# Two feed-forwards behind linear attention: the second up projection as seven block products for eight

## The chip, the cores and the metric

The kernel runs on one core of a Trainium2 chip. The metric is the device time of one execution in microseconds (us), the median of several runs. The core's engines run beside each other and each runs its own instructions in order: TensorE (PE; its weight loads are PEld), VectorE (DVE), ScalarE (ACT), GpSimd (POOL) and SyncE (SP), which issues the DMA transfers. They meet through semaphores.

## What is computed

Linear attention with a root-mean-square norm, then a gated feed-forward, then a second one with softplus:

```python
kv = np.einsum('bhsd,bhse->bhde', k, v)                  # 4 x 8 heads, 576 x 64
out = np.einsum('bhsd,bhde->bhse', q, kv)
x = (out / np.sqrt(np.mean(out * out, -1, keepdims=True) + 1e-06) * g_norm)   # 2304 x 512
g = x @ w_gate                                           # 512 x 1536
y = (g / (1 + np.exp(-g)) * (x @ w_val)) @ w_out         # 1536 x 512
h = y @ w_in                                             # 512 x 2048
z = (np.maximum(h, 0) + np.log1p(np.exp(-np.abs(h)))) @ w_out2    # 2048 x 512
```

The four weight matrices lie in DRAM as 8-byte numbers, two 4-byte words each.

## The kernel before

The 2304 tokens are five tiles: four of 512 columns, t = 0 to 3, and one of 256, t = 4 (the rest of every batch). Features lie on partitions. Every matrix product of the feed-forwards is made of three matmuls: each operand is kept as a high part and a low part in the float32r format, and `mm3` (L423) issues high by high, low by high and high by low.

Up projections contract 512 features in four steps (`up_proj`, L432: four `mm3` into one PSUM bank of the pool `ps`, five banks). Down projections go to the pool `po`, three banks, and VectorE adds each bank to an accumulator in SBUF (L486 `yacc`, L534 `zacc`); the bank is free when that add is done. In the first feed-forward `unit1(j, t)` (L624) is the unit of work: one block of 128 hidden features j (12 of them) by one token tile: four gate steps, four value steps, and between the last of these the four down steps of the unit before. Behind the value steps stands a chain: VectorE makes `u` (L465), ScalarE its high part `uh` (L468), VectorE its low part `ul` (L469); the next unit's first down step needs both. In the second feed-forward `unit2` (L635) takes two blocks j, j+1 and one token tile: 8 up steps, and 4 down steps of two blocks each, two units behind; softplus (L510) and `gh` (L511) are ScalarE's, `gl` (L512) GpSimd's.

A weight block comes by one DMA of 512 KB into one of five `stage` buffers and is turned by `split` (L253) in five steps: ScalarE L262, VectorE L265 and L266, VectorE L270, ScalarE L274, and the low part (L277) on GpSimd (first feed-forward) or VectorE (second). In the first feed-forward that is three blocks per j, in the second four per pair of j.

The order is written out by hand (`manual_schedule`): TensorE's order is that of the calls; `defer(dt, f)` puts work for the other engines into a list by planned time, and `tick` moves that time on with every `mm3` (0.216 us for a 512-column matmul) and issues what is due. So an instruction's place in its engine's row is set beforehand, at a place of TensorE's row.

## Time and profile before

| | us |
|---|---|
| median of three runs | 938.91 (938.23 to 939.47) |
| the profiled execution | 938.39 |
| its span, first to last instruction | 936.3 |
| TensorE busy | 905.9 |
| VectorE busy | 501.5 |
| ScalarE busy | 297.1 |
| GpSimd busy | 201.9 |

The span is the stretch of the profiled execution in which instructions ran; 2.1 us of its time lie around it. The first 160 us hold the loads and the attention, woven with the first two hidden blocks of the first feed-forward; from there to about 525 us the first feed-forward runs in a loop of 37 us per j, and from 525.6 to 922.9 us the second in a loop of 49 us per pair. A matmul's row shows its whole passage, 0.39 us for 512 columns, while the next one starts after 0.227 us: the distance between starts is what counts.

### The profile page before, as it was taken

To read this page: it belongs to the slowest core of one execution; us is meant where nothing else is said; L and a number is where in the kernel's file an instruction comes from. 1 tells how busy PE (TensorE), PEld (TensorE's weight loads), DVE (VectorE), ACT (ScalarE), POOL (GpSimd) and SP (SyncE) were. 2 spreads that over 40 slices of the span, in tenths; PEclk is the share of its full clock that TensorE was granted. 3 is DMA by queue.
4 is the path that set the end of the run, shared out by engine and by line. 5 is a ranking of instruction groups with operands and counts; after the bars stand their busy time and mean duration, and the time that the engine had idled before them with its cause. 6 is when DMAs were issued, how large, how long until landed. Compare 5 with 4: busy or idle time off the path is not lost.

```text
span 936.3 us, 11157 instructions
## 1 busy us (share of the span) xinstructions
PE 905.9 (97%) x4448; PEld 758.6 (81%) x4448; DVE 501.5 (54%) x805; ACT 297.1 (32%) x524; POOL 201.9 (22%) x164
## 2 busy tenths in 40 slices
PE   6899999999999999999999899999999999999994
PEld 5688887888888888888888788888888888888883
DVE  3945546665656656656657834443534443535222
ACT  3644343222222222222224633323232333233220
POOL 1722201100101111101014732222122222222220
PEclk9999999999999999999999999999999999999997
DMA  9973202201111111102010202111101020100022
...
DMA packets 58152, 55.25 MB, mean 59 GB/s; under 512 B 24692, under 2 KB 53364, under 8 KB 57716
## 3 DMA queue, kind: packets, MB, share of 16 engines
...
q14 instruction: 17, 0.14, 0.0%
q10 hardware_dynamic: 160, 0.00, 0.0%
...
## 4 chain that ended last, share of the span: by engine, by line
PE 89%; DVE 4%; SPq 2%; issue 2%; ACT 1%; DMA 1%; POOL 0%; POOLq 0%; DVEq 0%
PE pz L428 21%; PE ph L428 20%; PE pg L428 15%; PE pv L428 14%; PE py L428 14%; PE pa L358 1%; PE kvp L310 1%; DMA qr<-in_q_dram 1%; DVE yacc L486 1%; SPq L177 1%; PE px L389 1%; SPq L200 0%; PE pq L341 0%; DVE ul L469 0%; PE kvp L319 0%
## 5 line engine op out<-in xcount | busy, mean ns | idle before, releaser
L486 DVE TENSOR_TENSOR yacc<-yacc,py 128x512 f32<-128x512 f32 (+1 forms) x220 | 138.5, 631 | 98.9 <-PE py L428 98.3
L534 DVE TENSOR_TENSOR zacc<-zacc,pz 128x512 f32<-128x512 f32 x126 | 86.5, 687 | 189.0 <-PE pz L428 188.6
L512 POOL TENSOR_TENSOR gl<-l,gh 128x512 fp32r<-128x512 f32 (+1 forms) x80 | 96.6, 1208 | 280.7 <-ACT gh L511 161.7
L428 PE MATMUL ph<-yl,ih 128*128 128x512 f32 (+1 forms) x320 | 117.7, 368 | 0.0
L428 PE MATMUL ph<-yh,il 128*128 128x512 f32 (+1 forms) x320 | 117.7, 368 | 0.0
L428 PE MATMUL ph<-yh,ih 128*128 128x512 f32 (+1 forms) x320 | 117.6, 367 | 0.0
L510 ACT ACTIVATE l<-ph 128x512 f32<-128x512 f32 (+1 forms) x80 | 44.4, 555 | 228.1 <-PE ph L428 226.6
L428 PE MATMUL pz<-ph,gh 128*128 128x512 f32 x288 | 112.3, 390 | 0.0
L428 PE MATMUL pz<-pl,gh 128*128 128x512 f32 x288 | 112.3, 390 | 0.0
L428 PE MATMUL pz<-ph,gl 128*128 128x512 f32 x288 | 112.0, 389 | 0.0
L428 PE MATMUL py<-uh,oh 128*128 128x512 f32 (+1 forms) x240 | 90.3, 376 | 4.2 <-ACT uh L468 2.6
L468 ACT CAST uh<-u 128x512 fp32r<-128x512 f32 (+1 forms) x60 | 34.6, 577 | 176.6 <-DVE u L465 176.4
L428 PE MATMUL pg<-xh,gh 128*128 128x512 f32 (+1 forms) x240 | 90.1, 375 | 0.0
L428 PE MATMUL pv<-xh,vh 128*128 128x512 f32 (+1 forms) x240 | 89.8, 374 | 0.0
L428 PE MATMUL py<-ul,oh 128*128 128x512 f32 (+1 forms) x240 | 88.7, 370 | 0.8 <-DVE ul L469 0.8
L428 PE MATMUL pg<-xl,gh 128*128 128x512 f32 (+1 forms) x240 | 88.5, 369 | 0.3 <-DVE xl L396 0.3
L428 PE MATMUL py<-uh,ol 128*128 128x512 f32 (+1 forms) x240 | 88.7, 369 | 0.0
L428 PE MATMUL pv<-xh,vl 128*128 128x512 f32 (+1 forms) x240 | 88.6, 369 | 0.0
L428 PE MATMUL pg<-xh,gl 128*128 128x512 f32 (+1 forms) x240 | 88.5, 369 | 0.0
L428 PE MATMUL pv<-xl,vh 128*128 128x512 f32 (+1 forms) x240 | 88.4, 368 | 0.0
L428 PEld LDWEIGHTS ph<-yh,ih 128*128 128x128 f32 x320 | 60.2, 188 | 11.0
L428 PEld LDWEIGHTS ph<-yh,il 128*128 128x128 f32 x320 | 60.2, 188 | 10.8
...
## 6 DMA issues: line engine op xcount, KB each, us to landing
...
```

Of the source, the lines that this page charges most:

```text
L177: nc.sync.dma_start(kr.rearrange("p h c d -> p h (c d)"), ks.rearrange("h (p c) d -> p h (c d)", p=P))
L310: nc.tensor.matmul(pk[:, hp, :], lhsT=kt[:, c, i:i + 2, :].rearrange("p h d -> p (h d)"), rhs=vt[:, i:i + 2, c * D:(c + 1) * D], start=(c ...
L358: nc.tensor.matmul(pv[p0:p0 + n, hp, :], lhsT=qt[:, hp, p0:p0 + n], rhs=kvm[bb][:, hp, :], start=True, stop=True,)
L389: nc.tensor.transpose(px[:, hp, :], x[:, hp, :], ident)
L428: nc.tensor.matmul(dst, lhsT=a, rhs=b_, start=first and i == 0, stop=last and i == n - 1)
L468: nc.scalar.copy(uh, u)
L486: defer(ADD1, lambda: nc.vector.tensor_add(a[:, d, :], a[:, d, :], p))
L510: nc.scalar.activation(l, p, AF.Softplus)
L512: nc.gpsimd.tensor_sub(ul, l, f32(uh))
L534: defer(ADD2, lambda: nc.vector.tensor_add(av[:, m, :], av[:, m, :], p))
```

## The change

For each pair of hidden blocks (2jp, 2jp+1) and each pair of token tiles the second up projection is a 2 x 2 by 2 x 2 block product: the two hidden blocks by the two halves of the 512 input features (256 each), by the two token tiles. It was eight block products of 256 features; it is now seven (Strassen's scheme in Winograd's form), with sums of weight halves (`sums`), of token halves (`t_sum`) and of products. A product is `mm`: two `mm3`, six matmuls of 512 columns. Three PSUM banks X, Y, Z serve a pair: p6, p7, p3 and p4 add into a bank that already holds another product, and ScalarE (`copy`) or VectorE (`out_`) reads that bank first, in between.

The weight side: `pair2` converts the four weight blocks of a pair during the first feed-forward (j = 2 on, one pair every 40 planned us), makes four half-size sums on VectorE, and writes six blocks, high and low, to DRAM, 12 stores of 256 KB. `load2` reads them back before their use: once for tiles 0 and 1, and once more for tiles 2 and 3, since the second feed-forward now runs in two passes, n = 0 over tiles 0 and 1, n = 1 over tiles 2, 3 and the narrow one (`rest`, which keeps the plain product). The low parts are all GpSimd's.

The token side: `block` makes high (ScalarE) and low part (`BLO`: GpSimd for 0, 3, 4, 5; VectorE for 1, 2, 6) of seven 1,024-column blocks for each pair of tiles, and `t_sum` makes four sums on VectorE, in place in `yacc`. `blocks1` does that at the end of the first feed-forward in place of `yh`, `yl` of tiles 0 to 3; `blocks2` in the last pair of the first pass. The small SBUF pools become one pool `pages` of 12 buffers, plus 3 of the tag `rm`. The attention and the first feed-forward's matmuls stay.

```diff
-P2_AT = 14.36
-P2_EVERY = 8.29
-SPLIT2 = 3.88
+PAIR2 = 40.0
+STEP2 = 1.35
+LOAD2 = 8.0
...
+WLO2 = "gggggg"
+BLO = "gvvgggv"
...
-    remp = ctx.enter_context(tc.tile_pool(name="remp", bufs=1))
-    tp = ctx.enter_context(tc.tile_pool(name="tp", bufs=2))
-    cvp = ctx.enter_context(tc.tile_pool(name="cvp", bufs=2))
-    ap_ = ctx.enter_context(tc.tile_pool(name="ap", bufs=2))
+    pages = ctx.enter_context(tc.tile_pool(name="pages", bufs=12))
+    dram = ctx.enter_context(tc.tile_pool(name="dram", bufs=1, space=bass.MemoryType.DRAM))
...
-                (nc.gpsimd if YL[d] == "g" else nc.vector).tensor_sub(yl[:, d, :], a[:, d, :], f32(yh[:, d, :]))
-            if j == F1 - 1:
+                nc.gpsimd.tensor_sub(yl[:, d, :], a[:, d, :], f32(yh[:, d, :]))
...
+        def sums():
+            a, b = z["i", 0], z["i", 1]
+            z[1], z[2] = page("s12_"), page("s34_")
+            a11, a12, a21, a22 = a[:, :hw], a[:, hw:], b[:, :hw], b[:, hw:]
+            s1, s2, s3, s4 = z[1][:, :hw], z[1][:, hw:], z[2][:, :hw], z[2][:, hw:]
+            return [(s3, a11, a21, "-"), (s1, a21, a22, "+"), (s2, a22, s3, "-"), (s4, a12, s2, "-")]
...
+        def keep(i, key):
+            src = z[key]
+            hi = pages.tile([P, DM], F32R, tag="pg", name=f"kh{jp}_{i}")
+            z["h", i] = hi
+            nc.scalar.copy(hi, src)
+        def keep_lo(i, key):
+            src, hi = z[key], z["h", i]
+            lo = pages.tile([P, DM], F32R, tag="pg", name=f"kl{jp}_{i}")
+            (nc.gpsimd if WLO2[i] == "g" else nc.vector).tensor_sub(lo, src, f32(hi))
+            nc.sync.dma_start(w2d[jp][i][:, 0, :], f32(hi))
+            nc.sync.dma_start(w2d[jp][i][:, 1, :], f32(lo))
...
+        steps = conv("i", 0) + conv("i", 1) + [lambda i=i: add(i) for i in range(4)]
+        steps += kept(0, ("i", 0)) + kept(3, ("i", 1)) + kept(1, 1) + kept(2, 2)
+        steps += conv("p", 0) + kept(4, ("p", 0)) + conv("p", 1) + kept(5, ("p", 1))
+        for k_ in range(2):
+            defer(at - LOAD2 + 1.0 * k_, lambda k_=k_: load_cols(w2_in, "i", js[k_]))
+            defer(at + 10.0 + 6.0 * k_, lambda k_=k_: load_rows(w2_out, "p", js[k_]))
+        for k_, f in enumerate(steps):
+            defer(at + STEP2 * k_, f)
+    w2 = {}
+    def load2(jp):
+        for i in range(4):
+            if i < 2:
+                t = stage.tile([P, 2, DM], F32R, tag="stage", name=f"wh{jp}_{i}")
+                nc.sync.dma_start(f32(t), w2d[jp][i])
+                hl = t[:, 0, :], t[:, 1, :]
+            else:
+                hl = [wp.tile([P, DM], F32R, tag="ab"[i - 2] + "hl"[k_], name=f"wh{jp}_{i}{k_}") for k_ in range(2)]
+                for k_ in range(2):
+                    nc.sync.dma_start(f32(hl[k_]), w2d[jp][i][:, k_, :])
+            w2["h", jp, i] = hl
+        for i in range(2):
+            hl = [wop.tile([P, DM], F32R, tag="o" + "hl"[k_], name=f"wo{jp}_{i}{k_}") for k_ in range(2)]
+            for k_ in range(2):
+                nc.sync.dma_start(f32(hl[k_]), w2d[jp][4 + i][:, k_, :])
+            w2["o", jp, i] = hl
+    blk = {}
...
+    def block(n, i, tag, src):
+        def hi():
+            t = xp.tile([P, 2, KH, T], F32R, tag=tag, name=f"b{n}_{i}")
+            blk[n, i] = t
+            nc.scalar.copy(t[:, 0], src())
+        def lo():
+            t = blk[n, i]
+            (nc.gpsimd if BLO[i] == "g" else nc.vector).tensor_sub(t[:, 1], src(), f32(t[:, 0]))
+        return [hi, lo]
...
+    def t_sum(n, o, a, b):
+        def f():
+            h = halves(n)
+            nc.vector.tensor_sub(h[o], h[a], h[b])
+        return [f]
...
+    def block_steps(n, tags):
+        return [
+            block(n, 0, tags[0], half(n, 0)),
+            t_sum(n, 0, 2, 0) + block(n, 1, tags[1], half(n, 0)),
+            t_sum(n, 0, 3, 0) + block(n, 2, tags[2], half(n, 0)),
+            block(n, 3, tags[3], half(n, 1)),
+            t_sum(n, 2, 3, 2) + block(n, 4, tags[4], half(n, 2)),
+            block(n, 5, tags[5], half(n, 3)),
+            t_sum(n, 1, 1, 0) + block(n, 6, tags[6], half(n, 1)),
+        ]
+    TAGS1 = ["xh0", "xl0", "xh1", "xl1", "xh2", "xl2", "xh3"]
+    TAGS2 = ["xl3"] + TAGS1[:6]
+    def spread(steps, at, every):
+        return [(at + every * i, f) for i, f in enumerate(steps)]
+    def blocks1(t):
+        if t == 1:
+            s = block_steps(0, TAGS1)
+            blk["steps"] = s
+            return spread(s[0] + s[3], 0.5, 1.0)
+        if t == 2:
+            s = blk["steps"]
+            return spread(s[1] + s[2] + s[4] + s[5], 0.5, 0.6)
+        if t == 3:
+            return spread(blk["steps"][6], 0.9, 0.6)
+        return []
+    def blocks2():
+        s = block_steps(1, TAGS2)
+        r = spread(s[0], 0.2, 0.6)
+        for i in range(1, 7):
+            r += spread(s[i], 1.4 + 2.4 * (i - 1), 0.75)
+        return r
+    us2 = {}
+    served = count()
...
+    def quad(jp, t0, t1):
...
+        def mm(bank, i, first, a, c):
+            if first:
+                st[bank] = ps.tile([P, T], F32, tag="ps", name=f"h{bank}{jp}_{n}")
+            wh, wl = w2["h", jp, a]
+            b = blk[n, i]
+            mm3(st[bank], [
+                ((wh[:, (c + k_) * P:(c + k_ + 1) * P], wl[:, (c + k_) * P:(c + k_ + 1) * P]), (b[:, 0, k_], b[:, 1, k_]))
+                for k_ in range(KH)
+            ], first, True, check=False)
+        def copy(nm, bank):
+            st[nm] = pages.tile([P, T], F32, tag="rm", bufs=3, name=f"{nm}{jp}_{n}")
+            nc.scalar.copy(st[nm], st[bank])
+        def out_(nm, bank, other, k_, t):
+            st[nm] = page(f"{nm}{jp}_{n}")
+            nc.vector.tensor_add(st[nm], st[other], st[bank])
+            soft(2 * jp + k_, t, st[nm], st[nm], g_tiles())
+        def p1():
+            mm("Y", 0, True, 0, 0)
+            copy("p1", "Y")
+        def p5():
+            mm("Z", 1, True, 1, 0)
+            copy("p5", "Z")
+        def p6():
+            mm("Y", 2, False, 1, KH)
+            copy("u2", "Y")
+        def p2():
+            mm("X", 3, True, 0, KH)
+            out_("c11", "X", "p1", 0, t0)
+        def p7():
+            mm("Y", 4, False, 2, 0)
+            out_("c22", "Y", "p5", 1, t1)
+        def p3():
+            mm("Z", 5, False, 2, KH)
+            out_("c12", "Z", "u2", 0, t1)
+        def p4():
+            mm("Y", 6, False, 3, KH)
+            soft(2 * jp + 1, t0, st["Y"], page(f"c21{jp}_{n}"), g_tiles())
+        return [p1, p5, p6, p2, p7, p3, p4]
...
                 weave(unit1(1, t) + unit1(1, t + 1))
-        for j in range(2, F1):
-            if j + 1 < F1:
-                prepare(w1(j + 1), 10.0, P1_AT, P1_EVERY)
-            else:
-                prepare(w2(0), 12.0, 12.0, 6.0)
+        for jp in range(F2 // 2):
+            pair2(jp, jp * PAIR2)
+        for j in range(2, F1 - 1):
+            prepare(w1(j + 1), 10.0, P1_AT, P1_EVERY)
             for t in range(NT):
                 weave(unit1(j, t))
+        j = F1 - 1
+        load2(0)
+        for t in range(NT - 1):
+            weave(unit1(j, t))
+            for dt, f in blocks1(t):
+                defer(dt, f)
+        weave(ffn1_h(j, B))
         nc.scalar.preload_act_table_set("softplus")
-        behind += [[]] * (2 - LAG1)
-        for j in range(0, F2, 2):
-            if j + 2 < F2:
-                prepare(w2(j + 2), 10.0, P2_AT, P2_EVERY)
-            for t in range(NT):
-                weave(unit2(j, t))
-        for o in behind:
-            weave(o)
+        last = behind.pop(0)
+        for f in last + ffn1_o(j, B):
+            f()
+        late = []
+        for n, (t0, t1) in enumerate(((0, 1), (2, 3))):
+            for jp in range(F2 // 2):
+                if (n, jp) != (1, F2 // 2 - 1):
+                    load2((jp + 1) % (F2 // 2))
+                main = quad(jp, t0, t1)
+                if n == 0 and jp == F2 // 2 - 1:
+                    for dt, f in blocks2():
+                        defer(dt, f)
+                seq = []
+                for f in main:
+                    seq += [f] + late[:1]
+                    late = late[1:]
+                if n == 1:
+                    for f in rest(jp):
+                        seq += [f] + late[:1]
+                        late = late[1:]
+                for f in seq + late:
+                    f()
+                late = ffn2_o(jp, t1) + ffn2_o(jp, t0) + (ffn2_o(jp, B) if n == 1 else [])
+        for f in late:
+            f()
         flush()
```

Three places where the order of an engine moves. VectorE in the first feed-forward, from unit (6, 2) to (6, 3), before; `oz7` is a weight block of the first feed-forward, `py6_2_0` the first down bank of unit (6, 2):

```order
L486 TENSOR_TENSOR yacc1_875<-yacc1_875,py6_1_3_2842 128x512
L265 TENSOR_SCALAR oz7_2856<-oz7_2856 128x512
L266 SCALAR_TENSOR_TENSOR oz7_2856<-or7_2767,oz7_2856 128x512
L486 TENSOR_TENSOR yacc2_1146<-yacc2_1146,py6_2_0_2872 128x512
L270 SCALAR_TENSOR_TENSOR oz7_2856<-or7_2767,oz7_2856 128x512
L486 TENSOR_TENSOR yacc2_1146<-yacc2_1146,py6_2_1_2880 128x512
L486 TENSOR_TENSOR yacc2_1146<-yacc2_1146,py6_2_2_2889 128x512
L465 TENSOR_TENSOR u6_3_2898<-s6_3_2864,pv6_3_2866 128x512
```

The same place now; `zi8` and `zi9` are blocks of `w_in`, `s34_4` is a half-size sum:

```order
L493 TENSOR_TENSOR yacc1_918<-yacc1_918,py6_1_3_3173 128x512
L268 SCALAR_TENSOR_TENSOR zi8_3154<-ir8_3077,zi8_3154 128x512
L263 TENSOR_SCALAR oz7_3188<-oz7_3188 128x512
L264 SCALAR_TENSOR_TENSOR oz7_3188<-or7_3085,oz7_3188 128x512
L263 TENSOR_SCALAR zi9_3196<-zi9_3196 128x512
L264 SCALAR_TENSOR_TENSOR zi9_3196<-ir9_3090,zi9_3196 128x512
L493 TENSOR_TENSOR yacc2_1189<-yacc2_1189,py6_2_0_3206 128x512
L268 SCALAR_TENSOR_TENSOR oz7_3188<-or7_3085,oz7_3188 128x512
L268 SCALAR_TENSOR_TENSOR zi9_3196<-ir9_3090,zi9_3196 128x512
L493 TENSOR_TENSOR yacc2_1189<-yacc2_1189,py6_2_1_3216 128x512
L551 TENSOR_TENSOR s34_4_3231<-zi8_3154,zi9_3196 128x256
L493 TENSOR_TENSOR yacc2_1189<-yacc2_1189,py6_2_2_3226 128x512
```

Five instructions of the second feed-forward's weights now stand between the adds of these two units.

VectorE at the end of the first feed-forward (j = 11) before, from the end of unit (11, 1) on; `il0` and `iz1`, `pz0` belong to weights of the second feed-forward:

```order
L486 TENSOR_TENSOR yacc1_875<-yacc1_875,py11_1_3_4373 128x512
L277 TENSOR_TENSOR il0_4276<-iz0_4277,ih0_4275 128x512
L270 SCALAR_TENSOR_TENSOR iz1_4331<-ir1_4221,iz1_4331 128x512
L486 TENSOR_TENSOR yacc2_1146<-yacc2_1146,py11_2_0_4405 128x512
L265 TENSOR_SCALAR pz0_4397<-pz0_4397 128x512
L266 SCALAR_TENSOR_TENSOR pz0_4397<-pr0_4278,pz0_4397 128x512
L486 TENSOR_TENSOR yacc2_1146<-yacc2_1146,py11_2_1_4417 128x512
L486 TENSOR_TENSOR yacc2_1146<-yacc2_1146,py11_2_2_4430 128x512
L465 TENSOR_TENSOR u11_3_4440<-s11_3_4399,pv11_3_4401 128x512
```

The same place now; `b0_1` is a low part of a token block, the L622 rows are sums of 1,024 columns:

```order
L493 TENSOR_TENSOR yacc1_918<-yacc1_918,py11_1_3_4962 128x512
L622 TENSOR_TENSOR yacc0_644<-yacc1_918,yacc0_644 128x1024
L609 TENSOR_TENSOR b0_1_4975<-yacc0_644,b0_1_4975 128x1024
L622 TENSOR_TENSOR yacc0_644<-yacc1_918,yacc0_644 128x1024
L609 TENSOR_TENSOR b0_2_4991<-yacc0_644,b0_2_4991 128x1024
L622 TENSOR_TENSOR yacc1_918<-yacc1_918 128x1024
L493 TENSOR_TENSOR yacc2_1189<-yacc2_1189,py11_2_0_4993 128x512
L493 TENSOR_TENSOR yacc2_1189<-yacc2_1189,py11_2_1_5003 128x512
L493 TENSOR_TENSOR yacc2_1189<-yacc2_1189,py11_2_2_5014 128x512
L472 TENSOR_TENSOR u11_3_5025<-s11_3_4985,pv11_3_4987 128x512
L476 TENSOR_TENSOR ul11_3_5028<-u11_3_5025,uh11_3_5027 128x512
L493 TENSOR_TENSOR yacc2_1189<-yacc2_1189,py11_2_3_5031 128x512
```

Five 1,024-column instructions now stand ahead of the add that frees `py11_2_0`, and two more ahead of `u11_4`.

GpSimd in the second feed-forward before, where its row holds low parts of 512 or 256 columns alone:

```order
L512 TENSOR_TENSOR gl12_0_6799<-l12_0_6797,gh12_0_6798 128x512
L512 TENSOR_TENSOR gl13_0_6837<-l13_0_6835,gh13_0_6836 128x512
L512 TENSOR_TENSOR gl12_1_6875<-l12_1_6873,gh12_1_6874 128x512
L512 TENSOR_TENSOR gl13_1_6914<-l13_1_6912,gh13_1_6913 128x512
L512 TENSOR_TENSOR gl12_2_6935<-l12_2_6933,gh12_2_6934 128x512
```

GpSimd at the end of the first token pass now; `b1_0` to `b1_5` are low parts of token blocks of the second pass, `gl28` to `gl31` those of the last pair:

```order
L609 TENSOR_TENSOR b1_0_6224<-yacc2_1189,b1_0_6224 128x1024
L609 TENSOR_TENSOR b1_3_6268<-yacc2_1189,b1_3_6268 128x1024
L679 TENSOR_TENSOR gl28_6292<-c117_0_6289,gh28_6291 128x512
L609 TENSOR_TENSOR b1_4_6303<-yacc3_1314,b1_4_6303 128x1024
L679 TENSOR_TENSOR gl29_6318<-c227_0_6315,gh29_6317 128x512
L609 TENSOR_TENSOR b1_5_6313<-yacc3_1314,b1_5_6313 128x1024
L679 TENSOR_TENSOR gl30_6343<-c127_0_6340,gh30_6342 128x512
L679 TENSOR_TENSOR gl31_6364<-c217_0_6362,gh31_6363 128x512
```

The low parts that the next down projection reads now stand behind 1,024-column ones.

## Rows read from the trace of the kernel before

**Rows 1.** The page, busy time: us (share of span) xinstructions of each engine.
```profile
PE 905.9 (97%) x4448; PEld 758.6 (81%) x4448; DVE 501.5 (54%) x805; ACT 297.1 (32%) x524; POOL 201.9 (22%) x164
```

**Rows 2.** Chain that ended last, second feed-forward: start, us, engine, tile, line, matmuls.
```profile
600.40 4.08 PE ph L428 x18
...
611.28 2.15 PE ph L428 x18
```

**Rows 3.** Stretches: length, busy us (x) of PE, PEld, DVE, ACT, POOL, PEclk, DMA, GB/s.
```profile
345.00:382.00 37.00, 37.00 (x182) 31.28 (x182) 23.45 (x40) 9.22 (x16) 3.86 (x3) 1.00 0.13 43
493.00:530.00 37.00, 35.59 (x166) 28.91 (x165) 29.94 (x39) 17.90 (x32) 19.37 (x14) 1.00 0.14 43
628.00:677.00 49.00, 49.00 (x229) 41.01 (x228) 21.76 (x35) 15.83 (x28) 12.03 (x10) 1.00 0.14 43
```

**Rows 4.** Waits of TensorE from 520 us on: total us, times, longest.
```profile
PE py L428 <- DVE yacc L486: 1.6, 2, 1.3
PE py L428 <- ACT uh L468: 1.0, 1, 1.0
PE py L428 <- DVE ul L469: 0.2, 1, 0.2
```

**Rows 5.** Instructions by line and form: xcount | busy us, mean ns | idle before.
```profile
L486 DVE TENSOR_TENSOR yacc<-yacc,py 128x512 f32<-128x512 f32 x176 | 120.3, 685 | 63.4 <-PE py L428 62.8
...
L469 DVE TENSOR_TENSOR ul<-u,uh 128x512 fp32r<-128x512 f32 x48 | 34.9, 726 | 32.9 <-ACT uh L468 32.9
...
L468 ACT CAST uh<-u 128x512 fp32r<-128x512 f32 x48 | 29.8, 620 | 137.9 <-DVE u L465 137.8
...
L486 DVE TENSOR_TENSOR yacc<-yacc,py 128x256 f32<-128x256 f32 x44 | 18.2, 418 | 35.5 <-PE py L428 35.5
...
L277 POOL TENSOR_TENSOR gl<-gz,gh 128x512 fp32r<-128x512 f32 x12 | 15.6, 1297 | 181.4 <-ACT gh L274 181.4
...
L266 DVE SCALAR_TENSOR_TENSOR gz<-gr,gz 128x512 int32<-128x512 int32 x12 | 8.3, 693 | 0.4
...
L265 DVE TENSOR_SCALAR gz<-gz 128x512 int32<-128x512 int32 x12 | 5.1, 422 | 0.7 <-ACT gz L262 0.6
```

**Rows 6.** VectorE in order of time, one unit of the first feed-forward: start, us, [idle].
```profile
315.66 0.69 DVE L465 TENSOR_TENSOR u<-s,pv 128x512 f32<-128x512 f32 x1
317.04 0.69 DVE L469 TENSOR_TENSOR ul<-u,uh 128x512 fp32r<-128x512 f32 x1 [0.69 <-ACT uh L468]
317.64 0.68 DVE L486 TENSOR_TENSOR yacc<-yacc,py 128x512 f32<-128x512 f32 x1
...
320.35 0.69 DVE L486 TENSOR_TENSOR yacc<-yacc,py 128x512 f32<-128x512 f32 x1 [0.24 <-PE py L428]
321.71 0.69 DVE L486 TENSOR_TENSOR yacc<-yacc,py 128x512 f32<-128x512 f32 x1 [0.67 <-PE py L428]
...
323.82 0.69 DVE L465 TENSOR_TENSOR u<-s,pv 128x512 f32<-128x512 f32 x1
```

**Rows 7.** VectorE and GpSimd in order of time at the end of the first feed-forward.
```profile
508.06 3.07 POOL L491 TENSOR_TENSOR yl<-yacc,yh 128x512 fp32r<-128x512 f32 x2 [1.88 <-ACT yh L490]
...
508.30 1.67 DVE L266 SCALAR_TENSOR_TENSOR iz<-ir,iz 128x512 int32<-128x512 int32 x1
...
509.89 0.68 DVE L486 TENSOR_TENSOR yacc<-yacc,py 128x512 f32<-128x512 f32 x1
```

**Rows 8.** Stretches behind the last matmul, columns as in rows 3.
```profile
924.00:925.00 1.00, 0.00 (x0) 0.00 (x0) 0.00 (x0) 0.00 (x0) 0.00 (x0) 1.00 0.13 33
926.00:927.00 1.00, 0.00 (x0) 0.00 (x0) 0.00 (x0) 0.00 (x0) 0.00 (x0) 0.50 0.13 45
```

**Rows 9.** TensorE in order of time, first matmuls of the execution.
```profile
7.43 2.05 PE L310 MATMUL kvp<-v,k 128*128 128x128 f32 x8 [7.43 <-DMA v<-in_v_dram]
...
15.38 1.06 PE L310 MATMUL kvp<-v,k 128*128 128x128 f32 x8
```

**Rows 10.** One stretch of the opening loads, columns as in rows 3.
```profile
13.00:14.00 1.00, 1.00 (x6) 1.00 (x7) 0.52 (x1) 0.11 (x1) 0.00 (x0) 1.00 1.09 349
```

More of the change, by code (lines that the diff above doesn't have):

```diff
@@ L59 @@
 WLO1 = "g"
-WLO2 = "v"
 YL = "gggg"
-A0 = "v"
+WLO2 = "gggggg"
+BLO = "gvvgggv"
+GLO = "gggg"
 @with_exitstack
@@ L419, in attention_slots, with mm3 @@
         return kvs + pipe
-    def mm3(dst, steps, first=True, last=True, lo_rhs_last=True):
+    def mm3(dst, steps, first=True, last=True, lo_rhs_last=True, check=True):
         n = 3 * len(steps)
@@ L427, in mm3 @@
             for a, b_ in ((ah, bh), (al, bh), (ah, bl)) if lo_rhs_last else ((ah, bh), (ah, bl), (al, bh)):
-                nc.tensor.matmul(dst, lhsT=a, rhs=b_, start=first and i == 0, stop=last and i == n - 1)
+                nc.tensor.matmul(
+                    dst, lhsT=a, rhs=b_, start=first and i == 0, stop=last and i == n - 1,
+                    skip_group_check=not check)
                 i += 1
@@ new lines, in blocks2, with g_tiles, soft @@
+    def blocks2():
[6 more added lines that the diff above has]
+    served = count()
+    def g_tiles():
+        n = next(served)
+        pool, th, tl = (pages, "pg", "pg") if n % 7 > 3 else (up, "uh", "ul")
+        return pool.tile([P, T], F32R, tag=th, name=f"gh{n}"), pool.tile([P, T], F32R, tag=tl, name=f"gl{n}")
+    def soft(j, t, src, l, tiles, w=T, off=0):
+        hi, lo = (x[:, off:off + w] for x in tiles)
+        nc.scalar.activation(l, src, AF.Softplus)
+        nc.scalar.copy(hi, l)
+        nc.gpsimd.tensor_sub(lo, l, f32(hi))
+        us2[j, t] = hi, lo
@@ new lines, in rest, with step @@
+    def rest(jp):
+        st = {}
+        w = widths[B]
+        def step(k_, c):
+            if c == 0:
+                st[k_] = ps.tile([P, w], F32, tag="ps", name=f"hr{jp}_{k_}")
+                if k_ == 0:
+                    st["g"] = g_tiles()
+            wh, wl = w2["h", jp, 3 * k_]
+            yh, yl = xt["y", B]
+            mm3(st[k_], [((wh[:, c * P:(c + 1) * P], wl[:, c * P:(c + 1) * P]), (yh[:, c, :], yl[:, c, :]))],
+                c == 0, c == KD - 1)
+            if c == KD - 1:
+                soft(2 * jp + k_, B, st[k_], page(f"cr{jp}_{k_}", w), st["g"], w, k_ * w)
+        return [lambda k_=k_, c=c: step(k_, c) for k_ in range(2) for c in range(KD)]
```

119 lines of the change are left out of this document (64 added, 55 removed).

## The prediction

> **What bounds the kernel now.** I read the engines' busy time first, then stretches, then who waits. TensorE is busy for 97% of the span, the others for half of it or less [rows 1]. In the loop of the first feed-forward and in that of the second TensorE works through, 37.00 of 37.00 us and 49.00 of 49.00 [rows 3]. The chain that ended last runs through it: 18 matmuls of 512 columns take 4.08 us, 0.2267 us each, and 18 of 256 columns 2.15 us, 0.119 us each [rows 2]. So a matmul removed is worth its full 0.2267 us as long as TensorE stays fed. It starves in one place only, between the feed-forwards: from 493 to 530 us it is busy for 35.59 of 37 us [rows 3], and from 520 us on it waits 1.6 + 1.0 + 0.2 = 2.8 us for VectorE's adds, a high part and a low part [rows 4].
>
> **Removed from TensorE.** A pair of hidden blocks by a pair of token tiles took 2 x 2 x 4 x 3 = 48 matmuls of 512 columns and now takes 7 x 2 x 3 = 42. Over 8 pairs by 2 passes that is 96 matmuls, 96 x 0.2267 = **21.8 us** off the path. Nothing else on TensorE changes in number: the narrow tile and the down projections keep theirs. Everything below is what the change gives back.
>
> **First feed-forward: the weight side.** The loop takes 37 us per j; VectorE is busy 23.45 us of it [rows 3]. Its row has waits that no other work can fill: between `u` and `ul` it stands for ScalarE's high part, 317.04 - 315.66 - 0.69 = 0.69 us per unit [rows 6], some 3.2 us per j. `pair2` adds per pair four conversions of 0.42 + 0.69 + 0.69 = 1.80 us [rows 5] and four sums of 256 columns, 0.42 us each by the narrow add [rows 5]: 8.9 us per 40 planned us, which are 40 x 0.2267 / 0.216 = 42 real ones, so 7.8 us per j. 23.45 + 3.2 + 7.8 = 34.5 of 37 us: it fits, with little room.
>
> Does an instruction come late where TensorE needs it? In a wide unit `ul` is ready 2.1 us behind the last value step, and the first down step reads it 4.5 us behind (one down, four gate and one value step of three matmuls, 0.68 us each, and two matmuls): 2.4 us to spare. Ahead of the narrow tile it is 0.68 + 12 x 0.119 + 0.36 + 0.45 = 2.9 us: 0.8 to spare. I went down VectorE's new row adding 0.60 us for a 512-column instruction behind another (317.04 to 317.64, [rows 6]), 0.46 for the shift, 0.35 for a sum. In most units it is on time at `u`. In the densest, the place (6, 2) to (6, 3) shown with the change, unit (6, 1) hands over 0.9 us of lag, and `u6_3` starts 1.45 us late, just ahead of a narrow tile: TensorE would wait about 0.6 us there.
>
> That leaves VectorE and GpSimd in each other's way. At 508.06 GpSimd makes two low parts; a VectorE instruction with both inputs in SBUF starts at 508.30 and takes 1.67 us for 0.69; the add at 509.89, with one input in PSUM, takes 0.68 beside the second low part [rows 7]. So an SBUF-only instruction can lose about 1 us to a low part. In the loop now, with 3 low parts per j (3.86 us of GpSimd), nothing of that is visible; from 493 to 530 us, with 14 low parts, VectorE is busy 29.94 us for 39 instructions, 6.5 us more than the loop's 23.45 for 40 [rows 3]. The new loop has 3 + 6 x 37 / 42 = 8.3 low parts per j, between the two. TensorE's loss in the first feed-forward is then bounded by nothing (the loop of now) and 1.4 us per 37 us (493 to 530): 0 to 8.6 loops x 1.4 = 12 us. I take **4 us**, nearer to the loop, since VectorE is on time in most units.
>
> The Trainium skill (SBUF — State Buffer, Who interferes with whom) gives a rule against this part: VectorE and GpSimd share one port pair, held exclusively, so that handing low parts to GpSimd does not unburden VectorE. By that rule every low part that meets an SBUF-only instruction costs what [rows 7] show, and the time would be that of rival (b); the loop of now speaks against it, since its low parts fall beside adds from PSUM.
>
> The 12 stores per pair go to SyncE's queue between the weight loads and wait there for GpSimd's low part; loads come 8 to 10 us ahead, so that costs nothing, and the DMA engines are at 13% [rows 3].
>
> **Between the feed-forwards.** Here I count from the end of the last value step of unit (11, 2). A 1,024-column VectorE instruction is 0.685 + 2 x (0.685 - 0.418) = 1.22 us [rows 5], 1.13 behind another; in the same ratio ScalarE's is 0.62 x 1.78 = 1.1 and GpSimd's 1.297 x 1.78 = 2.3 us [rows 5]. VectorE: `ul` to 2.1, add 2.7, sum 3.8, high part on ScalarE 4.95, low part 6.1, sum 7.2, high part 8.35, low part 9.5, sum 10.6, and only then the add of `py11_2_0`, 11.3. TensorE wants that bank for `py11_2_3` at 8.16 (twelve steps): it waits 3.2 us. It then goes on to 14.9, the end of the narrow tile's 24 matmuls, and through three down steps to 17.0. VectorE: two adds 12.5, `u` 13.1, (ScalarE) `ul` 14.5, add 15.1, sum 16.2, (ScalarE) low part 18.5, `u11_4` 18.9, its `ul` 19.8, add 20.4. `py11_3_3` needs that bank: a second wait, 3.5 us. The rest goes at the pace of VectorE's adds, and the first block product starts at about 23.0 where an unhindered TensorE would be at 15.9: 7.1 us. If `ul11_3` and the last sum each meet one of GpSimd's 1,024-column low parts, as [rows 7] show for narrower ones, it is some 2.2 us more. 7.1 to 9.3, less the 2.8 us that the old passage waits [rows 4]: 4.3 to 6.5, I take **5.3 us**.
>
> The clock may join in. Behind the last matmul, at 922.9 us, the granted clock is 1.00 in the stretch 924 to 925 us and 0.50, the level of 1.2 GHz, from 926 on [rows 8]. The second wait, 3.5 to 5.5 us, is longer than the 3 us between. How long the lower level lasts behind a restart I can only bound: the first 8 matmuls of the execution take 2.05 us at 7.43, the same 8 take 1.06 us at 15.38 [rows 9], so up to some 7 us at half speed, 0 to 3.3 us lost. Part of that falls in steps that wait for VectorE anyway: **1.5 us**.
>
> **Second feed-forward.** A pair of the first pass is 90 matmuls, 20.4 us. ScalarE, VectorE and GpSimd have less to do per us than now. A product that adds into a used bank comes three steps of 1.36 us behind the one that it adds to (one product, two down steps), 4.1 us, for a read of 0.6 to 0.7 us: covered; in the first pair, without down steps, 1.36 us: covered still. At the end of the first pass `blocks2` adds seven 1,024-column instructions to VectorE, 8 us to its 7 in 20.4: it fits. GpSimd gets four, 9.2 us beside four of 1.3. Its row shows `gl30` behind the low part of block 5, which waits for ScalarE's high part behind product p7: I get 24.1 us from the start of the pair for `gl30`, and the next down step reads it at 22.5: 1.6 us, up to 4 with VectorE in the way. **2.2 us**.
>
> A pair reads 12 blocks of 256 KB, 3.15 MB in 20.4 us, 154 GB/s; the opening loads reach 349 GB/s [rows 10]. Buffers are free a pair ahead. I count nothing. The last down steps and stores are of the kind of now: nothing.
>
> **Sum.** -21.8 + 4 + 5.3 + 1.5 + 2.2 = -8.8 us. The profiled execution took 938.4 us, so 929.6; it lies 0.5 us below the median of the runs, so **930 us** for the median. With all low ends -16 us, 923; with all high ends 942.
>
> **Rivals.** (a) *Everything fits* (7%): neither the loop nor the passage loses more than now; about 938.9 - 21 = 918 us. For it: VectorE's idle time; against it: the two walks above.
>
> (b) *VectorE becomes the bound of the first feed-forward* (13%), the case on the other side. Its 34.5 us per j plus the hold-ups: 6.5 us for 14 low parts is 0.46 us each, and 8.3 of them make 3.9, 38.4 us for a loop of 37, 1.4 x 8.6 = 12 us; where other waits add to it, up to 15. Then -21.8 + 15 + 9 = +2, 941 us. It ends on the slow side when the first feed-forward loses over 13 us, 1.5 us per j. Against it: sums and shifts behind another start 0.09 us earlier than their durations say [rows 6], and few low parts in [rows 3]'s other loops collide.
>
> (c) *The weights come late* (4%): if only one load at a time moved, in the second feed-forward each pair would take longer than its 20.4 us; 1.8 us over eight pairs of the first pass gives 14 us, 944 us. Against it [rows 10].
>
> (d) *The shared banks serialise* (8%): 3 banks x 16 products wait 0.2 us for their reader, 9 us, 938 us: the saving does not arrive. Against it the 4.1 us of distance.
>
> The rest, 68%, is the forecast.
>
> **Chances.** Faster and slower begin 0.2% from 938.9 us, about what a measurement tells from no change: under 937.0, over 940.8. Faster 0.68 + 0.07 + 0.02 of (b) + 0.03 of (d) = 0.80; same 0.03 of (b) + 0.03 of (d) = 0.06; slower 0.08 + 0.04 + 0.02 = 0.14. The range 921 to 940 leaves out most of (a), half of (b) and (c).
>
> **What would show it.** In the new profile: TensorE's distance of 0.2267 us inside a pair; its idle time in the first feed-forward, for `ul` and `uh` ahead of narrow tiles (0 to 1.4 us per j); two waits of 3 to 5 us for `yacc` between the feed-forwards, with the granted clock behind them; one short wait for `gl` where the passes meet; no wait for a DMA and none of p6, p7, p3, p4 for `copy`. The forecast is wrong if the first feed-forward loses over 13 us or nothing, or if TensorE waits inside every pair.

## The result, and the profile after

The changed kernel takes **943.99 us** (median of 4 runs, 943.38 to 945.80), the kernel before 938.71 beside it: ratio 1.0059, interval 1.0041 to 1.0076. It is 0.6% slower where I had forecast 930 us. Its profiled execution took 943.84 us, with a span of 942.0, 5.7 us more than before.

The page's busy line shows that TensorE does lose the 96 matmuls and is 10.6 us less busy than in [rows 1]:

```profile
PE 895.3 (95%) x4352; PEld 744.5 (79%) x4352; DVE 555.2 (59%) x867; ACT 337.1 (36%) x586; POOL 263.3 (28%) x204
```

It stands still instead. In stretches (columns as in [rows 3]), four of the first feed-forward, the passage, and the end of the first pass:

```profile
197.00:234.00 37.00, 35.92 (x171) 29.38 (x170) 32.52 (x54) 12.70 (x23) 10.68 (x8) 1.00 0.38 132
308.00:345.00 37.00, 34.90 (x164) 28.50 (x163) 29.80 (x49) 13.18 (x24) 7.74 (x6) 1.00 0.43 145
345.00:382.00 37.00, 37.00 (x180) 31.04 (x179) 30.16 (x52) 14.11 (x26) 12.34 (x9) 1.00 0.64 213
456.00:493.00 37.00, 34.86 (x158) 28.57 (x157) 30.25 (x48) 12.63 (x23) 9.79 (x8) 0.95 0.46 157
530.00:579.00 49.00, 41.55 (x184) 34.54 (x183) 25.14 (x34) 21.05 (x33) 15.74 (x12) 0.93 0.25 86
677.00:726.00 49.00, 45.78 (x202) 37.59 (x201) 28.26 (x33) 22.19 (x33) 23.60 (x14) 1.00 0.36 129
```

VectorE is at 30 to 32.5 us of 37, for 23.45 in [rows 3], and the waits come and go: the third row has none. The longest, TensorE in order of time, with the idle time and its releaser at the end of the row:

```profile
344.44 0.51 PE L433 MATMUL py<-uh,oh 128*128 128x512 f32 x1 [2.01 <-ACT uh L475]
...
458.92 0.50 PE L433 MATMUL py<-uh,oh 128*128 128x512 f32 x1 [2.04 <-ACT uh L475]
...
537.45 0.50 PE L433 MATMUL py<-uh,oh 128*128 128x512 f32 x1 [3.46 <-DVE yacc L493]
548.51 0.79 PE L433 MATMUL py<-uh,oh 128*128 128x512 f32 x1 [3.65 <-DVE yacc L493]
...
710.46 0.50 PE L433 MATMUL pz<-wo,gl 128*128 128x512 f32 x1 [3.22 <-POOL gl L679]
```

Such rows alone understate the loss. So I laid the start of the same unit's first gate matmul in the two traces side by side. The last wide unit of the loop, (11, 3), starts at 509.43 us before and at 526.35 after; 0.68 us of this is there already at 124 us. That leaves **16.2 us** as the loop's loss, while the rows of waits in it add up to about 9 us. A wait of 0.69, 0.70 or 1.05 us delays the next unit by 0.95, 0.97 and 1.39, some 0.3 more: a matmul's row lasts 0.39 us at a distance of 0.2267, so the first part of a wait is hidden, and the first matmul behind it takes longer (0.50 us in the rows above). The wait of 2.04 us at 458 delays the next unit by 4.1 us, because the granted clock falls to 0.50 behind it, the level of 1.2 GHz:

```profile
458.00:459.00 1.00, 0.08 (x1) 0.08 (x1) 0.32 (x2) 0.75 (x2) 0.00 (x0) 1.00 0.15 53
459.00:460.00 1.00, 1.00 (x3) 0.57 (x4) 1.00 (x2) 0.67 (x2) 0.48 (x1) 0.90 0.03 10
460.00:461.00 1.00, 1.00 (x5) 0.91 (x5) 0.82 (x2) 0.00 (x0) 0.80 (x1) 0.50 0.70 262
...
463.00:464.00 1.00, 1.00 (x7) 0.82 (x7) 0.18 (x1) 0.00 (x0) 0.00 (x0) 0.90 0.96 298
```

The loss is not the same in each execution of one order of instructions. The kernels e4 and e6 below leave the loop as it is, and in their profiled executions it loses 17.8 us, since there the clock falls behind the wait at 344 us too. So the loop's loss in a single execution is read here to within 1.5 us.

The account of the span, each part measured from one matmul to another in both traces and set against bare matmuls (0.2267 and 0.119 us each; the passage has 84 of them, 15.2 us):

| part | lost before | lost after | change, us |
|---|---|---|---|
| 96 matmuls removed | | | -21.8 |
| loop of the first feed-forward | | | +16.2 |
| passage, from unit (11, 3) to the last down step | 4.7 | 10.8 | +6.1 |
| second feed-forward | 0.6 | 5.0 | +4.3 |
| opening and tail | | | +0.9 |
| sum (measured: +5.7) | | | +5.7 |

### The profile page after: what moved, and what is told of

Its sections match the earlier page's. It is cut to its first block, busy times and chain, and to the rows that moved or that the text cites. A ratio compares the mean times of both kernels' runs of the same rounds, so it can differ in the third digit from the quotient of the medians.

```text
span 942.0 us, 11753 instructions
## 1 busy us (share of the span) xinstructions
PE 895.3 (95%) x4352; PEld 744.5 (79%) x4352; DVE 555.2 (59%) x867; ACT 337.1 (36%) x586; POOL 263.3 (28%) x204
## 4 chain that ended last, share of the span: by engine, by line
PE 72%; DVE 17%; issue 4%; ACT 3%; POOL 2%; DMA 1%; SPq 0%; DVEq 0%; POOLq 0%; ACTq 0%
PE pz L433 21%; PE py L433 10%; PE pv L433 9%; PE pg L433 9%; PE hY L433 9%; PE hZ L433 4%; DVE yacc L493 3%; PE hr L433 2%; PE hX L433 2%; ACT uh L475 2%; DVE u L472 2%; DVE ul L476 1%; PE pa L363 1%; PE kvp L315 1%; DVE s L551 1%
## 5 line engine op out<-in xcount | busy, mean ns | idle before, releaser
L433 PE MATMUL pz<-wo,gh 128*128 128x512 f32 x576 | 177.9, 390 | 0.0
L493 DVE TENSOR_TENSOR yacc<-yacc,py 128x512 f32<-128x512 f32 (+1 forms) x220 | 135.4, 628 | 36.9 <-PE py L433 36.6
L679 POOL TENSOR_TENSOR gl<-c,gh 128x512 fp32r<-128x512 f32 x64 | 83.6, 1308 | 209.1 <-ACT gh L678 177.5
L433 PEld LDWEIGHTS pz<-wo,gh 128*128 128x128 f32 x576 | 106.7, 188 | 20.8
L433 PE MATMUL pz<-wo,gl 128*128 128x512 f32 x288 | 112.3, 390 | 3.6 <-POOL gl L679 3.6
L433 PE MATMUL hY<-b,wh 128*128 128x512 f32 x384 | 97.5, 390 | 0.0
L433 PEld LDWEIGHTS hY<-b,wh 128*128 128x128 f32 x384 | 71.6, 188 | 14.5
L433 PEld LDWEIGHTS py<-uh,oh 128*128 128x128 f32 x240 | 46.1, 192 | 27.2 <-DVE yacc L493 13.0
L433 PEld LDWEIGHTS pz<-wo,gl 128*128 128x128 f32 x288 | 54.1, 188 | 15.8 <-POOL gl L679 4.4
L476 DVE TENSOR_TENSOR ul<-u,uh 128x512 fp32r<-128x512 f32 (+1 forms) x60 | 42.4, 706 | 38.8 <-ACT uh L475 38.8
L677 ACT ACTIVATE c<-c 128x512 f32<-128x512 f32 x48 | 30.3, 632 | 86.6 <-DVE c L707 86.5
```

The source lines that it names most:

```text
L433: nc.tensor.matmul(dst, lhsT=a, rhs=b_, start=first and i == 0, stop=last and i == n - 1, skip_group_check=not check)
L476: (nc.gpsimd if UL1 == "g" else nc.vector).tensor_sub(ul, u, f32(uh))
L493: defer(ADD1, lambda: nc.vector.tensor_add(a[:, d, :], a[:, d, :], p))
L677: nc.scalar.activation(l, src, AF.Softplus)
L679: nc.gpsimd.tensor_sub(lo, l, f32(hi))
```

## What makes the loop late: a two by two

Why is `u`, and with it `uh`, late? VectorE's and GpSimd's rows ahead of the wait at 458 us:

```profile
450.88 0.42 DVE L263 TENSOR_SCALAR oz<-oz 128x512 int32<-128x512 int32 x1
451.33 1.72 DVE L264 SCALAR_TENSOR_TENSOR oz<-or,oz 128x512 int32<-128x512 int32 x1
452.98 0.67 DVE L493 TENSOR_TENSOR yacc<-yacc,py 128x512 f32<-128x512 f32 x1
...
455.83 1.19 DVE L268 SCALAR_TENSOR_TENSOR zp<-pr,zp 128x512 int32<-128x512 int32 x1
456.95 0.67 DVE L493 TENSOR_TENSOR yacc<-yacc,py 128x512 f32<-128x512 f32 x1
457.54 0.67 DVE L472 TENSOR_TENSOR u<-s,pv 128x512 f32<-128x512 f32 x1
```
```profile
451.20 1.30 POOL L562 TENSOR_TENSOR kl<-zp,kh 128x512 fp32r<-128x512 f32 x1 [5.03 <-ACT kh L557]
454.99 1.49 POOL L282 TENSOR_TENSOR ol<-oz,oh 128x512 fp32r<-128x512 f32 x1 [2.48 <-ACT oh L279]
```

VectorE runs without a pause from 449.06 to 458.2, and two of its instructions are 1.0 and 0.5 us longer than usual beside low parts of GpSimd. At the other long wait of the loop, 344 us, in the narrow unit of j = 6, it runs without a pause from 335.02 to 343.7, and a sum of weight halves takes 1.19 us for 0.42 beside a low part of the first feed-forward's own weights (VectorE, then GpSimd):

```profile
341.35 1.19 DVE L551 TENSOR_TENSOR s<-zi,zi 128x256 f32<-128x256 f32 x1
...
340.96 1.29 POOL L282 TENSOR_TENSOR ol<-oz,oh 128x512 fp32r<-128x512 f32 x1 [8.25 <-ACT oh L279]
```

**Theory A**: VectorE's added instructions by themselves make it late. **Theory B**: GpSimd's low parts hold them up. **Theory C**: neither (ScalarE's high parts, stores, loads). Three kernels take out one cause, the other, and both.

**Low parts out (e1).**

```
...
-            (nc.gpsimd if WLO2[i] == "g" else nc.vector).tensor_sub(lo, src, f32(hi))
...
-            nc.sync.dma_start(w2d[jp][i][:, 1, :], f32(lo))
+            nc.sync.dma_start(w2d[jp][i][:, 1, :], f32(hi))
```

> The six low parts per pair that GpSimd makes in the first feed-forward are left out; the high part is stored in both places, so the second feed-forward multiplies with wrong low parts at the same cost. VectorE's conversions and sums stay. In the changed kernel the start of the narrow tile's unit and of the next comes 16.2 us later at the end of the loop than in the kernel before (counted from 124 us on). Theory A (VectorE's own added instructions make it late): the loss stays at 13 to 16 us, the time at 941 to 944. Theory B (GpSimd's low parts hold up VectorE's instructions that read and write SBUF only): the loss falls to 3 to 6 us, the time to 931 to 934. Theory C (neither; ScalarE's high parts, the stores or the loads): 944.

**Conversions and sums out (e2).** `convert`'s first step alone is run, `add` does nothing.

```
-                z["f", nm, k_][i]()
+                if i == 0:
+                    z["f", nm, k_][i]()
...
-            (nc.vector.tensor_sub if op == "-" else nc.vector.tensor_add)(o, a, b)
+            z[1], z[2] = z["i", 0], z["i", 1]
```

> VectorE's part of the weight side is left out (shifts, sign and mantissa instructions of the four conversions per pair, and the four sums); ScalarE's and GpSimd's instructions, the loads and the stores stay, with wrong numbers in them. Theory A (VectorE's own added instructions): the loss of the first feed-forward falls from 16.2 to about 2 us, the time to 930. Theory B (GpSimd's low parts): the low parts still meet the conversions of the first feed-forward's own weights, 40 instructions per 37 us for some 58, so about half of the loss stays, 6 to 9 us, 934 to 937. Theory C: 944.

**Both out (e3).** The two edits together.

> Both are left out: VectorE's conversions and sums and GpSimd's low parts of the weight side; ScalarE's part, loads and stores stay. Theories A and B: the first feed-forward runs as in the kernel before, loss 0 to 1 us, the time 928; what is left then belongs to the passage between the feed-forwards and the end of the first pass, and 928 against 938.7 is what the block product itself brings. Theory C: the loss stays, 940 or more.

Measured, with the loop's loss from the profiled execution:

| | low parts on GpSimd | no low parts |
|---|---|---|
| conversions and sums | 944.0 us, loss 16.2 (the changed kernel) | 933.8 us, loss 3.6 (e1) |
| none | 928.0 us, loss -0.4 (e2) | 930.2 us, loss -0.4 (e3) |

C falls: with both out nothing is left. But A and B fall too, each as the only cause: A missed e1, B missed e2. The low parts alone cost nothing, the conversions alone 4 us, both 16. Why, VectorE's busy time shows. From the start of unit (2, 0) to that of (11, 3), with the columns of [rows 3], the changed kernel, e1, e2, e3, and e10 of further below:

```profile
153.12:526.35 373.23, 364.14 (x1730) 301.62 (x1729) 305.80 (x498) 130.63 (x232) 104.53 (x77) 1.00 0.46 155
153.45:514.04 360.59, 359.24 (x1729) 300.69 (x1728) 284.13 (x498) 131.24 (x232) 40.62 (x29) 1.00 0.48 161
153.22:509.83 356.61, 356.61 (x1730) 301.29 (x1728) 239.17 (x370) 131.40 (x232) 102.71 (x77) 1.00 0.48 163
152.02:508.63 356.61, 356.61 (x1729) 301.30 (x1728) 222.14 (x370) 131.07 (x232) 39.66 (x29) 1.00 0.49 163
154.80:522.96 368.16, 362.96 (x1729) 300.53 (x1728) 311.47 (x546) 130.46 (x232) 42.08 (x29) 1.00 0.47 158
```

The 48 low parts lengthen VectorE's work nearly as much without the conversions (239.2 us for 222.1) as with them (305.8 for 284.1), but TensorE pays only in the second case, where VectorE has little room to make up a delay. On average it still has some: 305.8 us and some 31 us of waits for `uh` are 337 of the 356.6 us that the loop takes unhindered, 34.9 of 37. But it goes up to 36.6 us without once waiting for TensorE, where in e1 the longest such stretch is 23.3 us and in the kernel before 5.2, and over so long a stretch lags can add up. So I read the loss as that of crowded stretches, and not of a row that is too long on average.

The instructions by line from 155 to 520 us show the price of one hold-up, first the changed kernel, then e1 (mean ns behind the busy time):

```profile
L264 DVE SCALAR_TENSOR_TENSOR vz<-vr,vz 128x512 int32<-128x512 int32 x9 | 10.1, 1123 | 0.3
...
L263 DVE TENSOR_SCALAR vz<-vz 128x512 int32<-128x512 int32 x9 | 7.6, 840 | 0.0
```
```profile
L264 DVE SCALAR_TENSOR_TENSOR vz<-vr,vz 128x512 int32<-128x512 int32 x9 | 6.2, 693 | 0.3
...
L263 DVE TENSOR_SCALAR vz<-vz 128x512 int32<-128x512 int32 x9 | 3.8, 420 | 0.0
```

All conversions and sums together take 147.2 us in the one and 126.5 in the other, the wide `ul` 3.1 us more: 24 us for 48 low parts, **0.5 us each**, as the 0.46 of the prediction said. In the profiled executions e3's second feed-forward is 4 us longer than e2's: within a wait of 3.3 us that ends at 693 us the granted clock falls to 0.50 for nearly 7 us, which it does not in e2's. The loop loses the same in both, so 930.2 against 928.0 says nothing on the loop.

**Low parts on VectorE (e10).** `WLO2 = "vvvvvv"`, nothing else.

> The changed kernel with one edit: the six low parts per pair of the weight side on VectorE in place of GpSimd. Theory B (hold-ups: 48 low parts cost VectorE about 0.49 us each beside its own conversions, 23 us over the loop; a low part of its own costs 0.69 us, but at a moment that nothing else is held up): the loss of the first feed-forward falls from 16.2 to 6 to 9 us, 934 to 938. Theory A (VectorE's row is full: 23.45 + 3.2 of waits + 7.8 + 3.6 = 38 of 37 us): the loss grows to 18 to 25 us, 946 to 953.

940.7 us (ratio to before 1.0016, 1.0006 to 1.0025), loss 12.6 in its profiled execution, the slowest of ten (943.1 us): between the two theories, and neither number. VectorE takes on more work (0.69 us for a low part) than it is relieved of (0.5 us), in all 311.5 us for 305.8 in the rows above, and still TensorE loses 3.6 us less. So a hold-up hurts more here than work of the same length; that it strikes at worse moments is my guess, since the edit also changes which instructions stand behind each other. Without the hold-ups the row still has too little room.

**Filled waits (e5).** Between `u` and `ul` VectorE waits 0.69 us for ScalarE, as in [rows 6]. A weight instruction due soon goes there.

```
             nc.scalar.copy(uh, u)
+            if not timed[0]:
+                fill(FILL)
             (nc.gpsimd if UL1 == "g" else nc.vector).tensor_sub(ul, u, f32(uh))
```

`fill(1.4)` takes from the queue of deferred steps the earliest VectorE step of a weight that is due within 1.4 planned us and has none of its own series ahead.

> VectorE waits 0.69 us for ScalarE's high part between u and ul. Here a weight instruction that is due within the next 1.4 planned us goes between them; 21 of the 46 wide and narrow units of the loop get one, nothing else moves. Theory (the row of VectorE has no room, so that each hold-up reaches TensorE): 21 x 0.69 = 14 us of row time come back, spread over the loop; its loss falls from 16.2 to 7 to 10 us, the time from 944 to 935 to 938. Rival: the instruction put ahead of ul (a shift and a sign step together take 1.1 us for 0.69) makes ul late where it has little room, ahead of narrow tiles; the loss stays, 942 to 946.

937.2 us, 0.9981 of before (0.9965 to 0.9997), its runs from 934.6 to 941.3; loss 8.3 in its profiled execution, one of the two fastest (934.8): as the theory had it. 1.6 us of room returned per 37 us halves the loss, as one would expect of a row with little room.

## The other two places

**Late blocks (e4).** In the pass boundary GpSimd's queue reads, in order of time:

```profile
699.99 1.30 POOL L679 TENSOR_TENSOR gl<-c,gh 128x512 fp32r<-128x512 f32 x1 [3.14 <-ACT gh L678]
701.24 3.39 POOL L609 TENSOR_TENSOR b<-yacc,b 128x1024 fp32r<-128x1024 f32 x1
704.59 2.29 POOL L679 TENSOR_TENSOR gl<-c,gh 128x512 fp32r<-128x512 f32 x1
706.84 2.35 POOL L609 TENSOR_TENSOR b<-yacc,b 128x1024 fp32r<-128x1024 f32 x1
709.15 2.50 POOL L679 TENSOR_TENSOR gl<-c,gh 128x512 fp32r<-128x512 f32 x2
```

Two of these take 1.0 us longer than their likes (3.39 us for 2.35, 2.29 for 1.30). VectorE has these beside them, so the delay goes both ways:

```profile
700.25 2.12 DVE L622 TENSOR_TENSOR yacc<-yacc 128x1024 f32<-128x1024 f32 x1
...
703.99 1.73 DVE L609 TENSOR_TENSOR b<-yacc,b 128x1024 fp32r<-128x1024 f32 x1 [1.03 <-ACT b L605]
```

What e4 changes:

```
-            r += spread(s[i], 1.4 + 2.4 * (i - 1), 0.75)
+            r += spread(s[i], 1.4 + 2.4 * (i - 1) + (11.9 if i > 3 else 0.0), 0.75)
```

> The last three token blocks of the second pass are made 11.9 planned us later, in the first pair of the second pass in place of the last pair of the first. Theory: the 3.2 us that TensorE waits for gl at 707 us come from GpSimd's low parts of blocks 4 and 5, of 2.4 to 3.4 us each, that stand ahead of gl on its queue; with them behind it the wait goes, and with the restart 3.5 to 4 us, 940. Rival: gl is late because of ScalarE's chain of softplus and high parts; the wait stays, 944. Second rival: the blocks now come too late for the fifth to seventh product, and a new wait of 1 to 3 us stands there, 942 to 944.

941.1 us, and the wait is gone: from the first block product to the second pair of the second pass it is 176.4 us for 179.8. No wait came in its place, so neither rival did; the loop's 17.8 us in this execution hide part of the gain.

**Passage spread (e6).** `blocks1(2)` makes blocks 1 and 2 only, `blocks1(3)` the rest.

```
-            return spread(s[1] + s[2] + s[4] + s[5], 0.5, 0.6)
+            return spread(s[1] + s[2], 0.5, 1.3)
...
-            return spread(blk["steps"][6], 0.9, 0.6)
+            s = blk["steps"]
+            return spread(s[5] + s[4], 0.5, 0.6) + spread(s[6], 5.0, 0.6)
```

> Between the feed-forwards VectorE takes blocks 1 and 2 over a whole unit, with TensorE's sums in between, and blocks 4 to 6 in the narrow unit and behind it. Theory: TensorE's two waits of 3.5 and 3.6 us are VectorE's, which stands through ScalarE's high parts (1.1 us each) with the adds queued behind; the passage loses 4 to 6 us in place of 10.5 (from the start of the last wide unit to the first block product), 938 to 940. Rival: the first block products now wait for their blocks, the loss only moves: 943 to 945.

944.7 us: a miss. The time is the rival's, but its mechanism did not come, since no block product waits for its block. The wait at 537 us is gone, and another took its place, for an add as before:

```profile
546.83 0.80 PE L433 MATMUL py<-uh,oh 128*128 128x512 f32 x1 [6.25 <-DVE yacc L493]
```

The passage got 1.5 us shorter (24.4 for 25.9), and in the loop the wait that the changed kernel has at 344 us, again 2.01 us long, was this time followed by the lower clock and delayed the next unit by 4.06 us for 2.67. The clock fell a second time at 710 us, where it had stayed up in the changed kernel, and the pair there took 28.2 us for 26.9. In this execution the two falls took back the gain.

**All three (e7)**, e4, e5 and e6 together:

> The filled waits, the spread passage and the late blocks of the second pass together. If the three losses are apart from each other, their gains add: 944 less 7, 4 and 3 us, 930, below the kernel before. If they share a cause (the clock behind a wait, or VectorE's lag carried from one to the next) the sum falls short: 934 to 940.

930.5 us (0.9911, 0.9894 to 0.9927): loop 8.4, passage 24.4, boundary without a wait. Part by part, in the profiled executions, the gains are those of the single edits: 7.9 us in the loop, 1.5 in the passage, 3.6 at the boundary. In that sense the three losses are apart. The medians do not add: alone the edits gained 6.8 (e5), 2.9 (e4) and -0.7 us (e6), 8.9 in all, where the three together gained 13.5. In e4's and e6's profiled executions the clock took part of the gain back, and e5's median lies 2.4 us above its profiled execution. So 930 came out as expected, but not from 7, 4 and 3.

**And the low parts on VectorE (e8)**, e7 with e10's edit:

> As the three together, and the six low parts per pair of the weight side on VectorE in place of GpSimd, 6 x 0.69 us per pair, 3.6 us per 37 us. Theory B in its strong form (the hold-ups are all that matters): no hold-ups, better than the three together, 926 to 930. Theory A (VectorE's row is full): 23.45 + 7.8 + 3.6 us of work and some 1.7 us of waits left are 36.6 of 37, so the row never recovers, the first feed-forward loses 8 to 15 us, 935 to 942.

926.5 us, loss 4.7: with the room that the filled waits give, the row bears 3.6 us more work, and the hold-ups by the 48 low parts are gone; those by the 29 low parts that GpSimd still makes in the loop stay. Theory A's sum of 36.6 of 37 us missed. What stays is the passage. There TensorE's one long wait stands behind two VectorE instructions beside GpSimd's low parts of blocks 4 and 5 (TensorE, GpSimd, VectorE; the lines' numbers have moved):

```profile
533.85 0.79 PE L446 MATMUL py<-uh,oh 128*128 128x512 f32 x1 [6.24 <-DVE yacc L508]
```
```profile
525.96 2.38 POOL L625 TENSOR_TENSOR b<-yacc,b 128x1024 fp32r<-128x1024 f32 x1 [13.54 <-ACT b L621]
530.57 2.34 POOL L625 TENSOR_TENSOR b<-yacc,b 128x1024 fp32r<-128x1024 f32 x1 [2.24 <-ACT b L621]
```
```profile
526.17 3.25 DVE L638 TENSOR_TENSOR yacc<-yacc 128x1024 f32<-128x1024 f32 x1
529.34 0.41 DVE L485 TENSOR_TENSOR u<-s,pv 128x256 f32<-128x256 f32 x1
530.83 2.36 DVE L491 TENSOR_TENSOR ul<-u,uh 128x256 fp32r<-128x256 f32 x1 [1.09 <-ACT uh L488]
```

The sum takes 3.25 us for 1.22, `ul` 2.36 for 0.42: each is done about its own usual length after GpSimd's instruction ends (528.3 and 532.9 us).

**Blocks 4 to 6 behind the narrow tile (e9)**: e8 with `blocks1(3)` as

```
+            return spread(s[4] + s[5] + s[6], 6.0, 0.4)
```

> As the kernel with all three and the low parts on VectorE (926.5), but blocks 4, 5 and 6 of the first pass are made 6 planned us behind the start of the last narrow tile, where the first block products begin. There the sum of 1,024 columns took 3.25 us beside block 4's low part on GpSimd, the narrow ul 2.36 beside block 5's, and TensorE waited 6.2 us, with the lower clock behind it. Theory (VectorE and GpSimd in each other's way in the passage): the passage falls from 24.4 to 16 to 18 us, against 15.4 of bare matmuls, 918 to 920. Rival: the fifth product now waits for its block, 3 us or more come back, 922 to 926.

922.5 us, above the theory's range and at the low end of the rival's: both came. The passage falls to 16.9 us, as forecast, but the first pair takes 12.7 us for 10.1, in two waits, one for `copy` and one for a block:

```profile
536.16 1.66 PE L446 MATMUL hY<-b,wh 128*128 128x512 f32 x6 [1.52 <-ACT p L720]
542.02 1.21 PE L446 MATMUL hZ<-b,wh 128*128 128x512 f32 x4 [1.04 <-POOL b L625]
```

The edit moves VectorE's sums and ScalarE's high parts along with GpSimd's low parts, so it does not tell the hold-ups in the passage from the work itself.

**Low parts as fillers too (e11)**: e9, with the low parts among the steps that `fill` may take.

> As the kernel before it in this list, but the low parts may also go between u and ul: 33 filled units for 21. Theory A for what is left of the loop's loss, 4.7 us (waits of VectorE's own row): 12 x 0.69 = 8 us of row time come back, the loss falls to 2 or 3 us, 2 us below the kernel before it in this list. Rival (what is left is the pairs of instructions ahead of ul): no change, within 1 us.

**921.3 us**, 0.9810 of before (0.9794 to 0.9827), loss 3.3 for 4.6: this version is 1.9% faster than the kernel before. Its step from e9, 1.2 us, lies between the theory's 2 and the rival's 1, and the two kernels' executions overlap (920.3 to 923.2 against 922.1 to 923.0), so it settles neither.

## Why the prediction was wrong

- **Removed, 21.8 us: right.** 4,352 matmuls for 4,448, six of a product in 1.36 us, and pairs of the second pass follow each other every 26.08 us, against 25.98 of bare matmuls.
- **First feed-forward, 0 to 12, taken as 4: this step failed.** It lost 16.2, more than the 13 that the prediction itself named as a sign of being wrong, and of the 14.5 us between the forecast -8.8 and the measured +5.7 it makes 12.2. What failed is the conclusion from "34.5 of 37 us: it fits", that a row with room on average costs TensorE little. The sum itself was near: with the hold-ups, which it left out, the trace has 34.9, since the rest came out shorter. But the room is not where the steps crowd, and there the walk down VectorE's new row used undisturbed durations: 0.60 us an instruction, 0.35 a sum, where the trace has 1.72 and 1.19 ahead of the wait at 458 us and 1.19 for a sum ahead of that at 344. The place was right: 344 us is where the walk had put a wait, in the narrow unit behind (6, 3), but 0.6 us was 2.01. Nor are the waits between `u` and `ul` such that "no other work can fill" them: e5 filled 21. Then a wait was priced at its idle time, without the 0.3 us of its restart and the lower clock, which I looked for in the passage alone. Rival (b) had added the hold-ups to the row (38.4 us, 12 to 15 lost, 941 us) and had 13%. Its cause was the right one, and "nearer to the loop of now" was no reason against it, since that loop has neither so many low parts nor so many instructions for them to meet. That its time comes so near is in part luck: a row of 38.4 of 37 us is not what the trace has. e1, e2 and e3 show that the loss needed both, low parts and conversions.
- **Passage, 5.3 and the clock 1.5: the sum right, in part by luck.** 6.1 us net, in two waits of 3.46 and 3.65 us for the adds (forecast 3.2 and 3.5). The clock's share was larger: it fell behind both waits (0.50 in the stretches from 539 to 541 and from 549 to 551 us), about 3 us each time, where I had one such fall. Against bare matmuls the new passage lost 10.8 us, for 9.6 in the forecast (2.8 + 5.3 + 1.5), but the old one had lost 4.7, and not the 2.8 of its rows of waits: again a wait priced at its idle time. The two shortfalls cancel in part.
- **End of the first pass, 1.6 to 4, taken as 2.2: right**, 3.5 us, for `gl` behind the low parts of blocks 4 and 5 (e4), with "VectorE in the way" for 2.0 of them.
- **Reloads, shared banks, tail at nothing: right.** No row of TensorE's waits names a DMA in the second feed-forward or `copy`, so rivals (c) and (d) did not occur; a wait of 0.3 us for `gl` in the first pair is new. In e9's order the first pair does wait 1.5 us for `copy`, so the cover that I counted there is not safe.
- **The Trainium skill's rule against this part**, that VectorE and GpSimd share one port pair held exclusively (the Trainium skill, SBUF — State Buffer, Who interferes with whom), I had weighed less than the loop of now. The trace agrees with it: the held-up instructions seem to begin when GpSimd's ends, adds that read PSUM keep their 0.68 us (64 of 512 columns beside a low part from 155 to 520 us, none over 0.69), and taking the low parts from GpSimd made the kernel faster though VectorE got more to do (e10, and e8 against e7). Handing a low part to GpSimd saved VectorE 0.69 us and cost it 0.5 on average.

Not settled: why the loop loses no more than 0.66 us from 349 to 455 us at the same rate of weight work (a pair every 40 planned us falls on other places of each loop of 35 planned us, but no run tested that); and 3 us or so of the loop's loss that are in no row of waits.
